# First batch laid out in memory already turned: its scores formed from the load, its other layout made on the chip

## The chip, the cores and the metric

The kernel runs on one core of a Trainium2 chip. The metric is the device time of one execution in microseconds (us), as the median of several executions. Five engines work from instruction queues of their own: PE (TensorE, matrix multiplies and turns), DVE (VectorE), ACT (ScalarE), POOL (GpSimd) and SP (SyncE, which here only issues transfers). Sixteen DMA engines move data between the chip's main memory and its SBUF.

## The reference

Eight batches of eight heads of attention between 512 tokens `x` and 32 states, in both directions, and then a soft mixture of eight experts over all 4608 rows.

```
scores  = scale * x @ state.T ;  a  = softmax(scores)  ; xread = a  @ state
scores2 = scale * state @ x.T ;  a2 = softmax(scores2) ; sread = a2 @ x
rows = concat(xread, sread), reshaped to (4608, 512)
logits = rows @ phi
slot_input = softmax(logits, over rows).T @ rows
slot_out[e] = relu(slot_input[e] @ w1[e]) @ w2[e]        # 8 experts, F = 1024
out = softmax(logits, over slots) @ slot_out
```

Everything is fp32. The weights are 32 MB of the some 42 MB that are read, and 8.9 MB are written.

## The kernel before

The attention is done one batch `b` at a time, and the batches overlap. The eight heads of a batch stand as four pairs `g`; `h` picks one of two halves. No scheduler decides the order: a hand-kept table `ORDER` lists steps by name (`X.0.1` is step `X` of batch 0, pair 1), each step issues its instructions when its turn comes, and every engine runs its own instructions strictly as they were issued. An instruction that waits holds up all that stand behind it on its engine.

The steps of one batch that matter here, with the lines of the kernel before:

- `X` (L228) turns one pair of the loaded `x` on PE (four 128x128 turns into a PSUM bank), and `xe` on ACT (L233) or `xd` on DVE (L238) copies the bank to SBUF times 0.125. The result is `xt`.
- `S` (L247) forms the scores of the batch on PE into two PSUM banks `sc` from the state and `xt`.
- First direction (softmax over the 32 states): `q` (DVE L260, a turn within 32x32 blocks out of `sc`), `m1` (DVE L265, maxima), `sub` (POOL L269), `x1` (ACT L272, exp), `l1` (DVE L276, sums), `rr` (DVE L281 and L282, one over the sums), `mul` (POOL L287), `aT` (DVE L292). Then `A`/`ae` turn and copy it, and `Lx` (PE L380) adds its logits.
- Second direction (softmax over the 512 tokens): `m2` (DVE L298, maxima out of `sc`), `e2` (ACT L303, exp with its sum), `E` (PE L311, a turn), `ee` on ACT or `ed` on DVE (L322, copy), `R` (PE L345, times `x` in its loaded layout), `sr` (DVE L358), `srT`, `srTe` (ACT) or `srTd` (DVE).
- `G` (PE L211) multiplies the states by `phi`, once for all batches. Its operand `phi_bd` is laid out by two copies on POOL (L203), which are issued ahead of the table and wait for the load of `phi`.
- `keep` copies logits out of PSUM, `V`/`Ve` turn and copy state results, `U`/`Ue` the states.

So `x` of a batch is used in two layouts: as loaded (tokens on partitions) by `R`, and turned by `S`. PSUM banks of `X`, `E`, `A`, `G` come from one pool of three (`ps_t`): a step that needs a bank waits for the copy that empties the one used three steps earlier.

SP issues the loads in one order: two of the four parts of `x` of batch 0 (256 KB each; ACT's queue issues the other two), the states of batches 0 and 1 (128 KB), `x` of batch 1 in two parts, the other states (384 KB), `phi` (64 KB), `x` of batches 2 to 7 (1 MB each), then the weights. `x` and weights share 13 SBUF buffers of 1 MB, and 4 of 2 MB hold weights; a weight that needs a buffer waits for the step that frees it (`load_w`).

After the attention come the experts: `w1` (PE L700), `w2` (PE L764), and the output (PE L800, copies on ACT L809 and DVE L810, stores issued by SP).

Of the kernel before, what the change touches and what calls it, by code (L numbers as in the profile page):

```python
# [35 lines left out]
l1.1.0 e2.2.0 R.1.0 sub.2.1 Lx.0.1 R.1.1 q.2.0 xe.3.2 X.3.3 rr.1 ae.0.0 A.0.1 X.4.3 e2.2.1 m1.2.0 sr.1 xe.3.3 S.3
xe.4.3 E.2.0 ae.0.1 mul.1.0 m2.3.1 aT.1.0 x1.2.1 X.4.0 mul.1.1 ee.2.0 X.4.1 E.2.1 xe.4.0 xe.4.1 q.3.1 X.4.2 sub.2.0
aT.1.1 srT.1 A.1.0 ee.2.1 x1.2.0 Lx.1.0 xe.4.2 R.2.0 Lx.1.1 R.2.1 m2.3.0 l1.2.1 l1.2.0 ae.1.0 mx.0 srTd.1 e2.3.0 mk.0
e2.3.1 X.5.2 keep.0 A.1.1 ae.1.1 rr.2 q.3.0 xe.5.2 sr.2 mul.2.1 E.3.0 bm.0 m1.3.0 nme.0 S.4 dx.0 X.5.0 ee.3.0 m1.3.1
sub.3.0 m2.4.1 aT.2.1 X.5.1 dT.0 E.3.1 m2.4.0 al.0 q.4.1 xe.5.0 dTe.0 x1.3.0 X.5.3 R.3.0 ee.3.1 T.0 e2.4.1 mul.2.0  # L40
aT.2.0 q.4.0 xe.5.3 Lu.0 R.3.1 srT.2 sub.3.1 m1.4.1 tt.0 sub.4.1 x1.3.1 xe.5.1 E.4.1 l1.3.0 A.2.0 l1.3.1 e2.4.0 m1.4.0
rr.3 x1.4.1 sub.4.0 X.7.2 Lx.2.0 ae.2.0 l1.4.1 ee.4.1 srTe.2 S.5 E.4.0 xe.7.2 X.7.1 sr.3 q.5.1 A.2.1 mul.3.0 ee.4.0
xe.7.1 ae.2.1 x1.4.0 m2.5.1 aT.3.0 m2.5.0 srT.3 X.7.3 srTe.3 xe.7.3 R.4.0 Lx.2.1 R.4.1 mul.3.1 aT.3.1 m1.5.1 sub.5.1
Lx.3.0 Ls.0 e2.5.0 X.7.0 e2.5.1 A.3.0 l1.4.0 q.5.0 Lse.0 E.5.0 rr.4 xe.7.0 Lr.0 A.3.1 x1.5.1 ee.5.0 ae.3.1 m1.5.0 S.7
msx.0 sub.5.0 dsx.0 sr.4 l1.5.1 ae.3.0 Lx.3.1 x1.5.0 mul.4.1 pv.1 m2.7.0 m2.7.1 R.5.0 l1.5.0 lkp.0 V.0 Ve.0 E.5.1 mx.1
ee.5.1 mul.4.0 rr.5 mul.5.1 U.0 srT.4 Ue.0 X.6.1 xe.6.1 X.6.0 R.5.1 srTd.4 q.7.1 mk.1 aT.4.0 sr.5 bm.1 nme.1 e2.7.0
xe.6.0 D.0 mul.5.0 aT.4.1 X.6.2 X.6.3 aT.5.0 E.7.0 srT.5 e2.7.1 xe.6.2 Px.0 xe.6.3 keep.1 q.7.0 m1.7.1 m1.7.0 E.7.1
ee.7.0 srTe.5 Y.0 S.6 Lx.4.0 sub.7.0 R.7.0 dx.1 m2.6.0 dT.1 ee.7.1 q.6.1 m2.6.1 aT.5.1 e2.6.0 sub.7.1 A.5.0 dTe.1
x1.7.0 m1.6.1 als.0 Lx.4.1 R.7.1 e2.6.1 al.1 q.6.0 Lx.5.0 T.1 x1.7.1 Lus.0 Lx.5.1 tt.1 windows E.6.0 ae.5.0 sub.6.1
keep.2 l1.7.0 m1.6.0 E.6.1 Ps.0 l1.7.1 Ys.0 A.4.0 ee.6.1 rr.7 ee.6.0 mx.2 sub.6.0 x1.6.1 pv.2 sr.7 A.5.1 l1.6.1  # L50
# [877 lines left out]
```

## Time and profile before

| | |
|---|---|
| time, median of 3 runs | 130.68 us (129.75 to 130.71) |
| time of the profiled execution | 130.03 us |
| its span, first to last instruction | 128.2 us |
| PE busy | 117.0 us (91%) |
| DVE busy | 86.4 us (67%) |
| ACT busy | 76.6 us (60%) |
| POOL busy | 44.8 us (35%) |
| moved by DMA | 51.74 MB, mean 404 GB/s |
| first instruction of the experts (PE L700) | at 76.11 us |

The span lies 1.83 us below the time of the same execution. Shares of busy time are means over three stages: the attention up to some 76 us, the experts up to some 100 us, and the output. The granted TensorE clock is 1.00 up to 122 us.

### The profile page before, as it was taken

The numbers are of one execution on the slowest core, as the hardware profiler recorded it, in microseconds if no ns is written. First come the engines' busy times: TensorE is split into PE (matmuls) and PEld (weight loads), VectorE is DVE, ScalarE is ACT, GpSimd is POOL, SyncE is SP. The second block draws the span as 40 slices with busy tenths as digits, with TensorE's granted clock in tenths as the row PEclk, the third lists the DMA queues.
The fourth block names the chain that finished last, engine by engine and source line by source line (L and its number), as shares of the span: only waits on it lengthen the run. The fifth ranks groups of instructions, "written<-read, shape, count | busy, mean of one in ns | idle before, by whom it ended". The sixth has DMA issues, their size and how long they took to land.

```text
span 128.2 us, 4689 instructions
## 1 busy us (share of the span) xinstructions
PE 117.0 (91%) x1984; PEld 81.2 (63%) x1984; DVE 86.4 (67%) x192; ACT 76.6 (60%) x187; POOL 44.8 (35%) x63
## 2 busy tenths in 40 slices
...
DVE  2329999999999999999985668029830346442600
...
DMA  3999999999999999999999999999999999999992
GB/s 138 396 409 430 419 429 419 429 419 427 419 422 427 419 427 424 419 427 422 427 422 429 419 415 409 431 414 434 414 447 414 414 380 413 432 399 416 373 414 105
DMA packets 8949, 51.74 MB, mean 404 GB/s; under 512 B 992, under 2 KB 1248, under 8 KB 4320
## 3 DMA queue, kind: packets, MB, share of 16 engines
...
q10 hardware_dynamic: 288, 0.52, 1.1%
...
## 4 chain that ended last, share of the span: by engine, by line
PE 70%; DVE 9%; DMA 7%; ACT 5%; issue 1%; DVEq 0%; POOL 0%; ACTq 0%; POOLq 0%
PE so_ps L764 12%; PE h_ps L700 11%; PE xt_ps L228 8%; PE o L800 7%; PE sc L247 5%; DMA phi_sb<-phi_in 5%; PE eT_ps L311 4%; PE sr_ps L345 4%; PE an_ps L311 3%; PE lt L380 3%; DMA x<-x_in 3%; PE t_ps L505 2%; DVE sums L276 2%; DVE q L260 2%; PE sum_ps L788 1%
## 5 line engine op out<-in xcount | busy, mean ns | idle before, releaser
L269 POOL TENSOR_TENSOR q<-q,m 128x512 f32<-128x512 f32 x16 | 16.8, 1051 | 15.6 <-DVE m L265 7.5
L233 ACT ACTIVATE xt<-xt_ps 128x512 f32<-128x512 f32 x30 | 17.9, 619 | 5.9 <-PE xt_ps L228 5.7
L228 PE MATMUL xt_ps<-ident,x 128*128 128x128 f32 x128 | 19.1, 291 | 0.0
L287 POOL TENSOR_TENSOR q<-q,rr 128x512 f32<-128x512 f32 x16 | 16.6, 1051 | 5.1 <-DVE rr L282 3.6
L810 DVE COPY out<-o 128x512 f32<-128x512 f32 x16 | 10.4, 686 | 11.5 <-PE o L800 11.4
L228 PEld LDWEIGHTS xt_ps<-ident,x 128*128 128x128 f32 x128 | 15.4, 150 | 3.0 <-ACT xt L233 0.8
L764 PE MATMUL so_ps<-w,h_m 128*32 128x128 f32 (+1 forms) x384 | 15.7, 310 | 0.0
L764 PEld LDWEIGHTS so_ps<-w,h_m 128*32 128x32 f32 x384 | 10.7, 110 | 7.4 <-issue 4.6
L700 PE MATMUL h_ps<-w,si_m 128*32 128x512 f32 x128 | 14.4, 594 | 0.1
L809 ACT COPY out<-o 128x512 f32<-128x512 f32 x16 | 8.7, 589 | 7.1 <-PE o L800 7.0
L298 DVE TENSOR_REDUCE nm<-sc 128x1 f32<-128x512 f32 x16 | 10.6, 671 | 2.7 <-PE sc L247 2.7
L700 PEld LDWEIGHTS h_ps<-w,si_m 128*32 128x32 f32 x128 | 9.1, 110 | 3.9 <-issue 2.9
L303 ACT ACTIVATE e<-sc,nm 128x512 f32<-128x512 f32 x16 | 11.3, 712 | 0.4 <-DVE nm L298 0.3
L260 DVE STREAM_TRANSPOSE q<-sc 128x512 f32<-128x512 f32 x16 | 11.1, 694 | 0.1
L292 DVE STREAM_TRANSPOSE aT<-q 128x512 f32<-128x512 f32 x16 | 10.9, 688 | 0.3 <-POOL q L287 0.2
L265 DVE TENSOR_REDUCE m<-q 128x16 f32<-128x512 f32 x16 | 10.4, 658 | 0.0
L276 DVE TENSOR_REDUCE sums<-q 128x16 f32<-128x512 f32 x16 | 10.4, 663 | 0.1
L272 ACT ACTIVATE q<-q 128x512 f32<-128x512 f32 x16 | 10.4, 649 | 0.1
L800 PE MATMUL o<-lt_all,so_r 32*128 32x512 f32 x64 | 10.2, 635 | 0.2 <-ACT out L809 0.2
L345 PE MATMUL sr_ps<-x,eT 128*32 128x64 f32 x512 | 10.4, 220 | 0.0
L311 PE MATMUL eT_ps<-ident,e 128*128 128x128 f32 x64 | 9.8, 279 | 0.0
L247 PE MATMUL sc<-xt,stT_sb 64*32 64x512 f32 x128 | 9.7, 601 | 0.0
...
## 6 DMA issues: line engine op xcount, KB each, us to landing
...
```

What stands on the lines that cost most here:

```text
L228: pe.transpose(p[:, P * j : P * j + P], xb[b][:, g, j, :], ident)
L233: act.mul(r[f"xt{g}"], r[f"xp{g}"], 0.125)
L247: pe.matmul(r[f"sp{h}"][32 * g : 32 * g + 32, :], st_t(b, g)[64 * h : 64 * h + 64, :], r[f"xt{g}"][64 * h : 64 * h + 64, :], start=True, s ...
L260: dve.transpose(r[f"q{h}"], r[f"sp{h}"])
L269: pool.tensor_tensor(v, v, R[b][f"m1{h}"].broadcast_to([P, 16, NS]), op=ALU.subtract)
L276: dve.tensor_reduce(out=v, in_=R[b][f"qv{h}"], axis=AX.X, op=ALU.add)
L287: pool.tensor_tensor(v, v, r.broadcast_to([P, 16, NS]), op=ALU.mult)
L311: pe.transpose(p[:, j, :], r[f"{src}{h}"][:, P * j : P * j + P], ident)
L345: pe.matmul(r["srp"][32 * g : 32 * g + 32, h, :], r[f"eT{h}"][:, j, 32 * g : 32 * g + 32], xb[b][:, g, j, D * h : D * h + D], start=(j == ...
L700: pe.matmul(h_ps[hf][32 * kt : 32 * kt + 32, :], si_m[kt // 2][:, 256 * (kt % 2) + 32 * e : 256 * (kt % 2) + 32 * e + 32], w1t[hf, e, kt], ...
L764: pe.matmul(so[k][32 * i : 32 * i + 32, :], h_m[hf][:, 256 * i + 32 * e : 256 * i + 32 * e + 32], w(i), start=(hf == 0 and e == 0), stop=( ...
L800: pe.matmul(o[j], so_r[hf][rows, col : col + 128], lt_all[rows, 4 * q : 4 * q + 4, :].rearrange("p b s -> p (b s)"), start=True, stop=True,)
```

## The change

Batch 0 is stored in main memory already turned (`x0T`: a pair's two heads times 64 on partitions, tokens along the row). A new step `S0` forms the scores of batch 0 from `x0T` as loaded, with states scaled by 0.125 on DVE (`st_s`); its first half takes pairs 0 and 1, its second pairs 2 and 3. The states of batches 0 and 1 are the first load, ahead of `x`. `X.0` turns `x0T` back, and `xe.0` copies it into a new SBUF buffer `x0`, from which `R.0` reads. That takes one of the 13 buffers, so one weight load fewer is issued ahead of the table, and the buffer of `x0T` takes that weight after the fourth `X.0`. A warm-up multiply `W0` on constants stands in front of the others. Copies by step: `xd` (DVE) goes from batch 0's pairs 1 and 0 to batch 1's pairs 3 and 2, batch 2's pair 1 and batch 6's pair 0; `ed.0.1` becomes `ee.0.1`, `keep.3` goes from ACT to DVE, `Ve.1` becomes `Vd.1`, `srTd` of batches 1 and 4 becomes `srTe`, and `srTe.0` becomes `srTd.0`. The whole table of steps is new.

```diff
 ORDER = """
-W.512 W.256 X.0.1 xd.0.1 X.0.0 xd.0.0 X.0.2 xe.0.2 X.0.3 xe.0.3 S.0 X.1.0 m2.0.1 X.1.2 X.1.1 xe.1.0 e2.0.1 xe.1.1
+W0.512 W.256 W.128 S0.0 S0.1 X.0.1 q.0.0 q.0.1 X.0.3 xe.0.1 X.0.0 xe.0.3 X.1.0 X.1.1 m1.0.0 m1.0.1 m2.0.0 sub.0.0
+xe.0.0 xe.1.0 m2.0.1 X.1.3 xe.1.1 X.1.2 sub.0.1 x1.0.0 xd.1.3 X.0.2 l1.0.0 e2.0.0 G.0 e2.0.1 G.3 G.1 x1.0.1 xd.1.2 G.2
...
     for b in range(B):
+        if b == 0:
+            nc.sync.dma_start(stT_sb[:, 0:1], st0)
+            x0T = big.tile([P, 4, S], F32, tag="big", name="x0T")
+            for i in range(4):
+                (act if i % 2 else nc.sync).dma_start(x0T[:, i], x0[i])
+            continue
         t = big.tile([P, 4, NJ, 2 * D], F32, tag="big", name=f"x{b}")
-        if b == 0:
-            for i in range(4):
-                v = x0[i].rearrange("p (g j c) -> p g j c", g=1, j=NJ)
-                (act if i % 2 else nc.sync).dma_start(t[:, 1 * i : 1 * i + 1], v)
-        elif b == 1:
+        if b == 1:
...
-        if b == 0:
-            nc.sync.dma_start(stT_sb[:, 0:1], st0)
...
+    xb.insert(0, big.tile([P, 4, NJ, 2 * D], F32, tag="big", name="x0"))
...
+    st_s = lt_all[:, B - 1, :].rearrange("p (a b n) -> p a b n", a=2, b=2)
+    dve.tensor_scalar_mul(st_s, stT_sb[:, 0, :, :, 0, :], 0.125)
...
             for j in range(NJ):
-                pe.transpose(p[:, P * j : P * j + P], xb[b][:, g, j, :], ident)
+                src = xb[b][:, g, j, :] if b else x0T[:, g, P * j : P * j + P]
+                pe.transpose(p[:, P * j : P * j + P], src, ident)
+            if b == 0:
+                r["turned"] = r.get("turned", 0) + 1
+                if r["turned"] == 4:
+                    load_w(1)
...
+        def xe(b, g, eng=act):
+            r = R[b]
+            if b == 0:
+                copy_of(eng)(xb[0][:, g].rearrange("p j c -> p (j c)"), r[f"xp{g}"])
+                return
...
+        def S0(i):
+            r = R[0]
+            for h in range(2):
+                if i == 0:
+                    r[f"sp{h}"] = ps_s.tile([P, S], F32, tag="sc", name=f"sc0_{h}")
+            for g in (2 * i, 2 * i + 1):
+                for h in range(2):
+                    pe.matmul(
+                        r[f"sp{h}"][32 * g : 32 * g + 32, :],
+                        st_s[64 * h : 64 * h + 64, g % 2, g // 2, :],
+                        x0T[64 * h : 64 * h + 64, g, :],
+                        start=True,
+                        stop=True,
+                    )
...
+        def first_warm(n):
+            p = ps_t.tile([P, S], F32, tag="tr", name="first_ps")
+            pe.matmul(p[:, 0:n], nc.const_aps.tensor(1.0, [P, P], F32), nc.const_aps.tensor(1.0, [P, n], F32), start=True, stop=True)
...
-        load_w(NBIG - B + 2 * NPAIR)
+        load_w(NBIG - B - 1 + 2 * NPAIR)
...
-        "x0_in": con(xl[0].reshape(P, 4, -1).transpose(1, 0, 2)),
+        "x0_in": con(x[0].reshape(4, 2, S, D).transpose(0, 1, 3, 2)).reshape(4, P, S),
```

How the instructions stand on three engines at the start of the attention follows, as they are issued, with what each waits for (PE, DVE, Activation and Pool are the engines; DMAHW is a transfer). `nm` is the result of `m2`, `m` of `m1`, `sums` of `l1`, `e` of `e2`.

DVE before, from its first work on data of batch 0:

```order
L238 TENSOR_SCALAR xt_1_165<-xt_ps_1_160 128x512 [waits PE_49]
L238 TENSOR_SCALAR xt_0_172<-xt_ps_0_167 128x512 [waits PE_49]
L298 TENSOR_REDUCE nm_0_1_203<-sc_1_189 128x1 [waits PE_49]
L260 STREAM_TRANSPOSE q_0_221<-sc_0_188 128x512
L298 TENSOR_REDUCE nm_0_0_242<-sc_0_188 128x1
L265 TENSOR_REDUCE m_0_0_252<-q_0_221 128x16 [waits DVE_49]
L260 STREAM_TRANSPOSE q_1_268<-sc_1_189 128x512 [waits Activation_49]
L265 TENSOR_REDUCE m_0_1_272<-q_1_268 128x16 [waits DVE_49]
L322 COPY eT_1_292<-eT_ps_1_259 128x512 [waits PE_49]
L276 TENSOR_REDUCE sums<-q_0_221 128x16 [waits Activation_49]
L298 TENSOR_REDUCE nm_1_0_312<-sc_0_282 128x1 [waits PE_49]
L260 STREAM_TRANSPOSE q_1_336<-sc_1_283 128x512 [waits PE_49]
```

DVE in the change, from its first work on scores of batch 0:

```order
L287 STREAM_TRANSPOSE q_0_177<-sc_0_162 128x512 [waits PE_49]
L287 STREAM_TRANSPOSE q_1_179<-sc_1_163 128x512 [waits PE_49]
L292 TENSOR_REDUCE m_0_0_203<-q_0_177 128x16 [waits DVE_49]
L292 TENSOR_REDUCE m_0_1_205<-q_1_179 128x16 [waits DVE_49]
L325 TENSOR_REDUCE nm_0_0_207<-sc_0_162 128x1
L325 TENSOR_REDUCE nm_0_1_213<-sc_1_163 128x1
L248 TENSOR_SCALAR xt_3_229<-xt_ps_3_215 128x512 [waits PE_49]
L303 TENSOR_REDUCE sums<-q_0_177 128x16 [waits Activation_49]
L248 TENSOR_SCALAR xt_2_269<-xt_ps_2_222 128x512 [waits PE_49]
L303 TENSOR_REDUCE sums<-q_1_179 128x16 [waits Activation_49]
L308 TENSOR_REDUCE rr_291<-sums 128x34 [waits DVE_49]
L309 RECIPROCAL rr_291<-rr_291 128x34 [waits DVE_49]
```

The two copies for batch 0 at the front are gone; both turns `q` and both `m1` come first; two copies for batch 1 (`xt_3`, `xt_2`) stand around the first `l1`, and both `l1` and `rr` of batch 0 stand ahead of all work on the scores of batch 1.

ACT before, from its first copy to the second exp of the first direction:

```order
L233 ACTIVATE xt_2_179<-xt_ps_2_174 128x512 [waits PE_49]
L233 ACTIVATE xt_3_186<-xt_ps_3_181 128x512 [waits PE_49]
L233 ACTIVATE xt_0_215<-xt_ps_0_198 128x512 [waits PE_49]
L303 ACTIVATE e_0_1_217,sums<-sc_1_189,nm_0_1_203 128x512 [waits DVE_49,Pool_49]
L233 ACTIVATE xt_1_219<-xt_ps_1_210 128x512 [waits PE_49]
L233 ACTIVATE xt_2_232<-xt_ps_2_205 128x512
L303 ACTIVATE e_0_0_264,sums<-sc_0_188,nm_0_0_242 128x512 [waits DVE_49]
L233 ACTIVATE xt_3_266<-xt_ps_3_254 128x512 [waits PE_49]
L272 ACTIVATE q_0_221<-q_0_221 128x512 [waits Pool_49]
L220 COPY G_sb<-g_ps 128x512 [waits PE_49]
L272 ACTIVATE q_1_268<-q_1_268 128x512 [waits Pool_49]
```

ACT in the change, from the same place:

```order
L242 COPY x_94<-xt_ps_1_172 128x512 [waits PE_49]
L242 COPY x_94<-xt_ps_3_181 128x512 [waits PE_49]
L242 COPY x_94<-xt_ps_0_187 128x512 [waits PE_49]
L246 ACTIVATE xt_0_211<-xt_ps_0_193 128x512 [waits PE_49]
L246 ACTIVATE xt_1_220<-xt_ps_1_198 128x512 [waits PE_49]
L299 ACTIVATE q_0_177<-q_0_177 128x512 [waits Pool_49]
L330 ACTIVATE e_0_0_239,sums<-sc_0_162,nm_0_0_207 128x512 [waits DVE_49]
L330 ACTIVATE e_0_1_250,sums<-sc_1_163,nm_0_1_213 128x512 [waits DVE_49]
L299 ACTIVATE q_1_179<-q_1_179 128x512 [waits Pool_49]
L224 COPY G_sb<-g_ps 128x512 [waits PE_49]
```

The first exp of the first direction, which waits for POOL, has moved ahead of both exps of the second direction, and the second one behind them.

POOL before, the two copies of `phi` and what stands behind them:

```order
L201 MEMSET phi_bd 128x256
L203 COPY phi_bd<-phi_sb 64x4x32 [waits DMAHW0_49,Pool_49]
L203 COPY phi_bd<-phi_sb 64x4x32
L269 TENSOR_TENSOR q_0_221<-q_0_221,m_0_0_252 128x512 [waits DVE_49,Pool_49]
L269 TENSOR_TENSOR q_1_268<-q_1_268,m_0_1_272 128x512 [waits DVE_49,PE_49]
```

POOL in the change, from the same place:

```order
L205 MEMSET phi_bd 128x256
L207 COPY phi_bd<-phi_sb 64x4x32 [waits DMAHW0_49,Pool_49]
L207 COPY phi_bd<-phi_sb 64x4x32
L296 TENSOR_TENSOR q_0_177<-q_0_177,m_0_0_203 128x512 [waits DVE_49,Pool_49]
L296 TENSOR_TENSOR q_1_179<-q_1_179,m_0_1_205 128x512 [waits DVE_49]
```

Nothing has moved there: the copies of `phi` stand in front of the first `sub` of batch 0 in both kernels.

## Rows read from the trace of the kernel before

**Rows 1.** The page of the profile, busy tenths in 40 equal slices of the span (3.2 us each), for VectorE and for the 16 DMA engines.

```profile
DVE  2329999999999999999985668029830346442600
...
DMA  3999999999999999999999999999999999999992
```

**Rows 2.** The view by windows, five stretches of the attention: window in us, its length, then busy us (and instructions) of PE, PEld, DVE, ACT and POOL, the granted TensorE clock, the busy share of the DMA engines, GB/s.

```profile
20.00:30.00 10.00, 10.00 (x216) 7.90 (x204) 9.70 (x19) 9.69 (x22) 5.55 (x6) 1.00 1.01 424
30.00:40.00 10.00, 10.00 (x219) 7.67 (x209) 9.93 (x23) 9.93 (x26) 5.49 (x7) 1.00 1.01 424
40.00:50.00 10.00, 10.00 (x210) 8.02 (x203) 9.93 (x23) 9.82 (x26) 6.98 (x7) 1.00 1.01 424
50.00:60.00 10.00, 9.98 (x232) 7.75 (x231) 9.86 (x24) 9.65 (x28) 5.80 (x9) 1.00 1.01 423
60.00:65.00 5.00, 4.68 (x95) 3.44 (x94) 4.83 (x15) 4.36 (x13) 4.25 (x5) 1.00 1.02 428
```

**Rows 3.** The chain of work that ended last, in order of time: start us, us, what.

```profile
3.97 6.09 DMA phi_sb<-phi_in
...
10.87 0.88 PE g_ps L211 x48
...
12.33 0.44 PE eT_ps L311 x4
...
13.13 1.07 PE sc L247 x16
...
64.45 0.30 DVE sr L358
...
70.82 0.27 ACT lt_all L390
...
76.11 9.06 PE h_ps L700 x80
```

**Rows 4.** The timeline of VectorE: start us, us, engine, line, operation, output and input, shapes, count, and in brackets the idle time before and what ended it.

```profile
5.18 0.69 DVE L238 TENSOR_SCALAR xt<-xt_ps 128x512 f32<-128x512 f32 x1 [2.89 <-PE xt_ps L228]
6.03 0.69 DVE L238 TENSOR_SCALAR xt<-xt_ps 128x512 f32<-128x512 f32 x1 [0.16 <-PE xt_ps L228]
...
9.12 0.69 DVE L298 TENSOR_REDUCE nm<-sc 128x1 f32<-128x512 f32 x1 [2.40 <-PE sc L247]
...
14.27 0.69 DVE L298 TENSOR_REDUCE nm<-sc 128x1 f32<-128x512 f32 x1
14.87 0.70 DVE L260 STREAM_TRANSPOSE q<-sc 128x512 f32<-128x512 f32 x1
15.50 0.64 DVE L276 TENSOR_REDUCE sums<-q 128x16 f32<-128x512 f32 x1
...
17.25 0.21 DVE L281 TENSOR_REDUCE rr<-sums 128x34 f32<-128x68 f32 x1
17.50 0.37 DVE L282 RECIPROCAL rr<-rr 128x34 f32<-128x34 f32 x1
17.79 0.66 DVE L260 STREAM_TRANSPOSE q<-sc 128x512 f32<-128x512 f32 x1
...
30.69 0.28 DVE L369 COPY srT<-srT_ps 128x128 f32<-128x128 f32 x1
30.88 0.21 DVE L281 TENSOR_REDUCE rr<-sums 128x34 f32<-128x68 f32 x1
```

**Rows 5.** The timeline of all engines, the same columns, rows of ScalarE and GpSimd between 10 and 14 us.

```profile
10.19 0.68 ACT L303 ACTIVATE e<-sc,nm 128x512 f32<-128x512 f32 x1
10.20 0.62 POOL L203 COPY phi_bd<-phi_sb 64x128 f32<-64x128 f32 x2 [8.49 <-DMA phi_sb<-phi_in]
...
10.86 1.09 ACT L233 ACTIVATE xt<-xt_ps 128x512 f32<-128x512 f32 x2
...
11.75 1.05 POOL L269 TENSOR_TENSOR q<-q,m 128x512 f32<-128x512 f32 x1 [0.94 <-DVE m L265]
...
12.95 0.67 ACT L272 ACTIVATE q<-q 128x512 f32<-128x512 f32 x1
...
13.47 0.62 ACT L220 COPY G_sb<-g_ps 128x512 f32<-128x512 f32 x1
```

**Rows 6.** The view of the transfers, issues by line: what, queue, operation, count, KB each, median us from issue to landing; and from the timeline the start of the issue of the states.

```profile
stT_sb<-st_in SPq DMA_DIRECT2D x1, 128.0 KB, 4.3
phi_sb<-phi_in SPq DMA_DIRECT2D x1, 64.0 KB, 6.1
...
1.63 0.42 SPq L98 DMA_DIRECT2D stT_sb<-st_in  x1
```

**Rows 7.** The timeline of TensorE: sixteen turns of batch 0, twelve of batch 1, and the scores of batch 1.

```profile
4.08 3.21 PE L228 MATMUL xt_ps<-ident,x 128*128 128x128 f32 x16
...
9.01 1.53 PE L228 MATMUL xt_ps<-ident,x 128*128 128x128 f32 x12
...
13.06 1.14 PE L247 MATMUL sc<-xt,stT_sb 64*32 64x512 f32 x16
```

**Rows 8.** The view by windows again, same columns as rows 2: four stretches from the first stores to the last.

```profile
100.00:105.00 5.00, 5.00 (x102) 2.97 (x102) 2.47 (x4) 2.41 (x5) 0.00 (x0) 1.00 0.94 397
105.00:110.00 5.00, 5.00 (x86) 2.94 (x88) 2.68 (x5) 2.57 (x6) 0.00 (x0) 1.00 0.99 408
...
115.00:120.00 5.00, 4.39 (x50) 2.35 (x42) 1.96 (x5) 2.72 (x8) 0.00 (x0) 1.00 0.94 383
120.00:122.00 2.00, 0.39 (x2) 0.00 (x0) 1.26 (x2) 1.00 (x2) 0.00 (x0) 1.00 1.02 418
```

More of the change, by code (lines that the diff above doesn't have):

```diff
@@ L36 @@
[L36 to L50, printed above, removed]
@@ new lines @@
+ae.0.1 aT.1.1 E.2.0 S.3 sr.1 sub.2.0 ee.2.1 X.4.0 sub.2.1 X.4.2 x1.2.0 srT.1 ee.2.0 aT.1.0 srTd.0 m2.3.0 l1.2.0 A.1.1
+x1.2.1 xe.4.0 X.4.1 l1.2.1 m2.3.1 Lx.1.0 q.3.1 xe.4.2 e2.3.0 ae.1.1 R.2.0 Lx.1.1 rr.2 xe.4.1 R.2.1 X.4.3 mx.0 srTe.1
+e2.3.1 xe.4.3 q.3.0 sr.2 mul.2.1 E.3.0 mul.2.0 mk.0 ee.3.0 A.1.0 E.3.1 m1.3.0 srT.2 aT.2.1 sub.3.0 bm.0 nme.0 S.4
+X.5.3 ae.1.0 aT.2.0 m1.3.1 keep.0 ee.3.1 q.4.1 m2.4.0 X.5.0 X.5.1 dx.0 x1.3.0 xe.5.3 srTe.2 sub.3.1 xe.5.1 dT.0 q.4.0
+m2.4.1 dTe.0 X.5.2 R.3.0 Lx.2.0 m1.4.0 x1.3.1 xe.5.0 m1.4.1 l1.3.0 l1.3.1 R.3.1 e2.4.0 sub.4.0 rr.3 e2.4.1 sr.3 Lx.2.1
```

41 lines of the change are left out of this document (25 added, 16 removed).

## The prediction

> **What bounds the kernel now.** I read the page's slices first. The DMA engines are full from the second slice to the last but one, and DVE is full from about 9 us until past 60 us [rows 1]. The windows say it closer: from 20 to 65 us DVE is busy 9.70 to 9.93 of every 10 us and 4.83 of the last 5, while PE (as the profile models it) and ACT stand nearly as high [rows 2]. The idle time of DVE in these 45 us is 0.30 + 0.07 + 0.07 + 0.14 + 0.17 = 0.75 us. So in the attention the time is the work that DVE has, plus the moment at which it starts; whatever is added to DVE, or left idle on it early, arrives almost undiminished at 65 us. The chain of waits agrees at its turning point: DVE's `sr` at 64.45 us releases the tail of the attention, and `w1` starts at 76.11 us [rows 3].
>
> At the end a second bound stands close by. The first store follows the last load so closely that the DMA engines are busy 0.94 of 100 to 105 us, 0.99, later 0.94, and 1.02 [rows 8]. A delay of the first store leaves them idle for as long, and the end moves with it. An advance gains only what they now miss: 5 x 0.06 + 5 x 0.01 + 5 x 0.06 = 0.65 us. By bytes, against the 424 GB/s of the attention [rows 2], the same three windows miss 5 x (27 + 16 + 41) / 424 = 1.0 us. These two are the bounds of any gain.
>
> **What the change gives.** Before, DVE has two copies at 5.18 and 6.03 us and then idles 2.40 us until the scores are there at 9.12 us [rows 4]. After, the scores need only the loads. The same five transfers must land; the last of them landed at 1.63 + 4.3 = 5.93 us [rows 6], now it is a part of `x0T`. Behind it stands half of `S0`. A whole `S` takes 1.14 us, and early work of PE runs at about half the later pace (16 turns in 3.21 us against 12 in 1.53 us [rows 7], at a granted clock of 1.00), so half costs 0.6 to 1.1 us. DVE gets its first `q` at 6.5 to 7.0 us; I take 6.8, 2.3 us earlier. The scaling of the states on DVE and `W0` lie in the wait for the loads and cost nothing; without that cover each would cost under 1 us, which the next step hides as well.
>
> **What takes it back: POOL.** The first `sub` needs `m1`, but on POOL the two copies of `phi` stand ahead of it, before and after. `phi` is issued at 3.97 us and lands 6.09 us later, at 10.06 us [rows 3]; the copies take 0.62 us from 10.20 us [rows 5]. The change moves no bytes from in front of `phi` to behind it. So `sub` starts at about 10.85 us, against 11.75 before. Before, little was queued behind this wait: ACT and DVE had `e2`, `m2` and copies to do. After, they have not:
>
> - DVE runs `q`, `q`, `m1`, `m1`, `m2`, `m2` and one copy at a pitch of 0.60 us (14.27, 14.87, 15.50 [rows 4]), from 6.8 to 11.0 us. Next in its queue is `l1.0.0`, which needs `x1.0.0`, which needs `sub`: 10.85 + 1.05 + 0.52 = 12.45 us (1.05 of `sub`; 0.52 is `x1` at 12.95 to the next at 13.47 [rows 5]). DVE idles 1.45 us.
> - Behind `l1.0.0` stands the copy of `xt` of batch 1, pair 2, from 13.05 to 13.7 us, and PE's scores of batch 1 wait for it. They run 13.75 to 14.9 us; before, they ended at 13.06 + 1.14 = 14.20 us [rows 7].
> - ACT has `x1.0.0` ahead of both `e2` now. So `x1.0.1` waits for two `e2` of 0.67 us each (10.19 to 10.86 [rows 5]): 12.45 + 1.35 + 0.52 = 14.35 us. Then `l1.0.1` can go, then `rr`, and at 15.5 us the first turn on scores of batch 1. DVE idles another 0.7 us in front of `l1.0.1`.
>
> If the cover is priced the other way: with `sub` free to go when `m1` is there (8.65 us), the same walk puts `l1.0.0` at 11.0 us without idling and the first turn of batch 1 at 13.4 us. The wait for `phi` is worth 2.1 us of DVE's time.
>
> **The ledger at 15.5 us.** Before, DVE starts `l1.0.1` at 15.50 us and has `m2.1.0` and a `q` of batch 1 behind it [rows 4]. After, it has done `l1.0.1` (0.60) and `rr` (17.25 to 17.79, 0.54 [rows 4]) which before had not; it still owes `m2.1.0` and that `q` (1.20), and two copies `xd` that before sat on ACT (batches 2 and 6: 1.20); it is spared one `srTd` (30.69 to 30.88, 0.19 [rows 4]). Sum: 1.20 + 1.20 - 0.60 - 0.54 - 0.19 = 1.07 us more work, from the same moment on, on an engine with 0.75 us of idle time in the rest. PE gives the same: its scores of batch 1 end 0.7 us later and one turn of 0.44 us [rows 3] that was done before is still owed, 1.1 us. ACT owes about the same as before, and is later spared some copies; it doesn't set the end.
>
> The rest of the change: the four `X.0` and their four copies exist in both kernels; their later use, `R.0`, comes after `S.1` in both. The buffer that `x0` takes costs one weight load issued ahead, which now waits for the fourth `X.0`, about 10.5 us, while SP's queue reaches it far later, with all of `x` and twelve weights in front of it; no cost, and up to the 2.4 us by which a megabyte fills the engines at 424 GB/s if that cover were gone. In the tail `keep.3` leaves ACT, where it takes 0.27 us of the chain [rows 3]: -0.27. `Vd.1` falls into DVE's slack behind 65 us [rows 1]. The experts and the output are untouched.
>
> **Sum.** 1.07 - 0.27 = +0.8 us at the start of the experts, and as much at the end. The profiled execution of before took 130.03 us, 0.65 below the median; the three runs and it have a mean of 130.3 us. By the profiled one alone 130.8 us, by the median 131.5 us; I go from the mean: 131.1 us.
>
> [...] The row says that 64 KB of `phi` took 6.1 us to land where 128 KB of states issued earlier took 4.3 us [rows 6]. [...]
>
> **Rivals.**
>
> *Faster: POOL is not held.* If `phi` lands by 8.0 us, `sub` is free at `m1`'s end and the 2.1 us come back: DVE ends 1.05 us earlier than before, the experts start 1.3 us earlier, and the DMA engines let through 0.65 to 1.0 us: 129.3 to 129.65 us, I write 129.5. For it: the states in front are small, and the page doesn't show why a transfer lands when it does. Against: the same bytes stand in front of `phi`. Chance 0.17.
>
> *No difference.* The table is new throughout; behind batch 1 it may fill the 0.75 us of idle time, or batch 0's early `m1` may spare later waits. It would give 130.3 us. For it: three engines share the load almost evenly [rows 2], so an order can shift work; ACT has the room. Against: DVE has nothing to fill. The case that the early scores change nothing at all lies here too. Chance 0.23.
>
> *More stalls.* Four copies on DVE now hold PSUM banks for PE, and each stands behind a reduction that waits for POOL or ACT. The two that I walked cost 1.45 and 0.7 us; a further one (batch 2, pair 1, before `S.2`) costs about one `sub`, 1.05 us: 132.1 us. It decides from the point at which `S.2` waits for that copy. Chance 0.20.
>
> *The forecast*, +0.3 to +1.5 us, 130.6 to 131.8 us: 0.40.
>
> **Chances and range.** About 1% (1.3 us) is what a measurement can tell from no change: under 129.4 is faster, over 132.0 slower. Faster is a good half of the first rival, 0.10. Slower is most of the stalls and a tail of the forecast, 0.22. The rest, 0.68, is within 1%. The range goes from the first rival's 129.5 to 132.5, the stalls with some of their spread; it leaves out under a tenth on each side.
>
> **What would show it.** Right: DVE's first `q` near 6.8 us; POOL's first `sub` still at 10.8 us behind `phi`; an idle time of DVE over 1 us in front of the first `l1` and a second one in front of the next; scores of batch 1 not earlier than before; DVE's last `sr` about 1 us later, `w1` starting near 76.9 us. Wrong: `phi` landing at 9 us or earlier, or DVE without idle time between 7 and 15 us; `w1` starting before 76 us; or a start of `w1` that moves without the end moving, which would put the bound into the DMA engines instead.

## The result and the profile after

| | before | after |
|---|---|---|
| median, 20 runs each | 130.31 us (129.52 to 131.73) | 131.19 us (130.60 to 131.58) |
| time of the profiled execution | 130.03 us | 131.54 us |
| its span | 128.2 us | 129.8 us |
| VectorE busy | 86.4 us | 88.1 us |
| first instruction of the experts | 76.11 us | 78.11 us |

The changed kernel takes 1.0069 of the time before, 95% interval 1.0047 to 1.009: slower by 0.9 us in the medians, which the 1% of the prediction counts as no change. The two profiled executions stand further apart, 1.51 us: that of before is 0.28 us under its median, that of after 0.35 us over its own. Ratios here and below leave out three executions in a slower state, one of e1 and two of e2, which the medians of those two runs include.

VectorE (DVE) after, its timeline from the first work on scores to the first turns of batch 1, then its last `sr` (columns as in [rows 4]):

```profile
8.07 1.31 DVE L287 STREAM_TRANSPOSE q<-sc 128x512 f32<-128x512 f32 x2 [3.95 <-PE sc L260]
9.30 1.24 DVE L292 TENSOR_REDUCE m<-q 128x16 f32<-128x512 f32 x2
10.46 1.28 DVE L325 TENSOR_REDUCE nm<-sc 128x1 f32<-128x512 f32 x2
11.65 0.68 DVE L248 TENSOR_SCALAR xt<-xt_ps 128x512 f32<-128x512 f32 x1
13.17 0.69 DVE L303 TENSOR_REDUCE sums<-q 128x16 f32<-128x512 f32 x1 [0.84 <-ACT q L299]
13.78 0.68 DVE L248 TENSOR_SCALAR xt<-xt_ps 128x512 f32<-128x512 f32 x1
15.03 0.69 DVE L303 TENSOR_REDUCE sums<-q 128x16 f32<-128x512 f32 x1 [0.57 <-ACT q L299]
15.75 0.22 DVE L308 TENSOR_REDUCE rr<-sums 128x34 f32<-128x68 f32 x1
16.00 0.37 DVE L309 RECIPROCAL rr<-rr 128x34 f32<-128x34 f32 x1
16.29 1.25 DVE L287 STREAM_TRANSPOSE q<-sc 128x512 f32<-128x512 f32 x2
...
66.08 0.29 DVE L385 TENSOR_TENSOR sr<-sr_ps,rr 128x128 f32<-128x128 f32 x1
```

The scores reach DVE 1.05 us earlier than the 9.12 us of [rows 4]. Then the two idle times that were forecast stand in front of the two `l1`, 0.84 and 0.57 us, and the turns of batch 1 start at 16.29 us. The last `sr` is 1.63 us later than in [rows 3].

What the two idle times wait for, first on GpSimd (POOL), then on ScalarE (ACT), timelines of after:

```profile
10.72 0.61 POOL L207 COPY phi_bd<-phi_sb 64x128 f32<-64x128 f32 x2 [9.02 <-DMA phi_sb<-phi_in]
11.43 2.06 POOL L296 TENSOR_TENSOR q<-q,m 128x512 f32<-128x512 f32 x2
```

```profile
12.51 0.63 ACT L299 ACTIVATE q<-q 128x512 f32<-128x512 f32 x1 [0.64 <-POOL q L296]
13.05 0.67 ACT L330 ACTIVATE e<-sc,nm 128x512 f32<-128x512 f32 x1
...
13.71 0.68 ACT L330 ACTIVATE e<-sc,nm 128x512 f32<-128x512 f32 x1
...
14.37 0.62 ACT L299 ACTIVATE q<-q 128x512 f32<-128x512 f32 x1
```

POOL does nothing until `phi` is there, although DVE had done both `m1` by 10.54 us; the first `sub` follows the copies at 11.43 us. The second exp of the first direction stands behind both of the second direction.

TensorE (PE), timeline of after: the scores of batch 0 from the load, and those of batch 1.

```profile
5.31 2.68 PE L260 MATMUL sc<-x0T,lt_all 64*32 64x512 f32 x16 [1.21 <-DMA x0T<-x_in]
...
13.86 1.76 PE L274 MATMUL sc<-xt,stT_sb 64*32 64x512 f32 x16 [0.25 <-ACT e L330]
```

The new step takes 2.68 us. The scores of batch 1 start 0.80 us later than before [rows 7].

The windows of after, columns as in [rows 2] and [rows 8]:

```profile
20.00:30.00 10.00, 9.76 (x174) 7.04 (x164) 9.96 (x21) 9.35 (x22) 5.59 (x6) 1.00 1.01 424
30.00:40.00 10.00, 10.00 (x231) 8.23 (x233) 9.81 (x20) 10.00 (x28) 4.88 (x5) 1.00 1.01 424
40.00:50.00 10.00, 10.00 (x202) 7.12 (x199) 9.76 (x24) 9.81 (x25) 6.29 (x7) 1.00 1.01 421
50.00:60.00 10.00, 10.00 (x196) 7.75 (x195) 9.96 (x23) 9.10 (x26) 5.40 (x7) 1.00 1.01 425
60.00:65.00 5.00, 4.80 (x137) 3.61 (x136) 4.97 (x13) 4.91 (x11) 2.98 (x3) 1.00 1.01 423
100.00:105.00 5.00, 4.78 (x88) 2.80 (x80) 1.58 (x3) 1.87 (x5) 0.00 (x0) 1.00 0.84 357
...
115.00:120.00 5.00, 4.62 (x79) 2.69 (x70) 1.29 (x2) 1.98 (x5) 0.00 (x0) 1.00 1.00 408
```

DVE now idles 0.54 us of the 45 (0.04 + 0.19 + 0.24 + 0.04 + 0.03), against 0.75 before: no slack is left for a late start. In the output the first stores come later (0.84 of 100 to 105 us where it was 0.94 in [rows 8]), and the stretch before the end, 0.94 before, is now full.

The chain of after, in order of time:

```profile
4.05 6.54 DMA phi_sb<-phi_in
...
66.47 2.06 POOL q L314 x2
68.56 0.72 DVE aT L319
...
78.11 9.06 PE h_ps L731 x80
```

It starts from `phi`, as that of before did [rows 3]. New in it are two `mul` on POOL, which start 0.39 us behind the last `sr`; that `sr`, on which the chain of before turned, does not stand in it, since the pair waits for a copy on ACT (L361). From `sr` to the experts it is 12.03 us, where it was 11.66.

### The profile page after: what moved, and what is told of

Read it like the earlier page. It is cut to its first block, busy times and chain, and to the rows that moved or that the text cites. A ratio compares the mean times of both kernels' runs of the same rounds, so it can differ in the third digit from the quotient of the medians.

```text
span 129.8 us, 4693 instructions
## 1 busy us (share of the span) xinstructions
PE 118.2 (91%) x1986; PEld 80.5 (62%) x1986; DVE 88.1 (68%) x195; ACT 75.8 (58%) x185; POOL 44.7 (34%) x63
## 4 chain that ended last, share of the span: by engine, by line
PE 46%; DVE 28%; DMA 8%; ACT 5%; POOL 3%; issue 3%; DVEq 0%; ACTq 0%; POOLq 0%
PE so_ps L795 11%; PE h_ps L731 11%; PE o L831 7%; DVE q L287 6%; DVE nm L325 5%; DVE sums L303 5%; DMA phi_sb<-phi_in 5%; DVE aT L319 4%; DVE m L292 4%; DMA x0T<-x_in 3%; PE an_ps L338 2%; PE sc L274 2%; POOL q L296 2%; POOL q L314 2%; PE t_ps L532 2%
## 5 line engine op out<-in xcount | busy, mean ns | idle before, releaser
L233 PE MATMUL xt_ps<-ident,x 128*128 128x128 f32 x112 | 15.4, 278 | 0.0
L246 ACT ACTIVATE xt<-xt_ps 128x512 f32<-128x512 f32 x24 | 14.0, 607 | 0.2 <-DVE aT L319 0.2
L233 PEld LDWEIGHTS xt_ps<-ident,x 128*128 128x128 f32 x112 | 12.3, 140 | 2.5 <-ACT lt_all L417 0.8
L372 PEld LDWEIGHTS sr_ps<-x,eT 128*32 128x32 f32 x512 | 8.4, 110 | 2.0 <-issue 1.5
```

What stands on the lines that cost most here:

```text
L233: pe.transpose(p[:, P * j : P * j + P], src, ident)
L372: pe.matmul(r["srp"][32 * g : 32 * g + 32, h, :], r[f"eT{h}"][:, j, 32 * g : 32 * g + 32], xb[b][:, g, j, D * h : D * h + D], start=(j == ...
```

## The experiments

The theory taken to the chip: DVE's full stretch hands on any delay, and what the early scores bring is taken back (1) by POOL, which holds the first `sub` behind the copies of `phi`, and (2) by the copies that the change adds to DVE. Rivals: (3) the scores are simply not early enough, because PE is slow in the new step; (4) the loss sits in the order of DVE's copies around `l1`; (5) it sits in the tail. Every ratio is to the kernel before on the same chip; the changed kernel was timed in the first comparison only, so an edit of it is set against it through the two ratios. The columns after the ratio are of the profiled execution, in us. "First turn" is the start of batch 1's first `q` in kernels with the change, and of `l1.0.1` in the others, the moment from which the prediction made its ledger; "stretch" is from there to the last `sr`.

| run | median | ratio (95%) | DVE's first work on scores | first `sub` | first turn | last `sr` | stretch | experts | span |
|---|---|---|---|---|---|---|---|---|---|
| before | 130.31 | 1 | 9.12 | 11.75 | 15.50 | 64.45 | 48.95 | 76.11 | 128.2 |
| after | 131.19 | 1.0069 (1.0047 to 1.009) | 8.07 | 11.43 | 16.29 | 66.08 | 49.79 | 78.11 | 129.8 |
| e1_phi_early | 130.77 | 1.0026 (0.9992 to 1.0059) | 8.07 | 10.11 | 15.12 | 64.92 | 49.80 | 76.93 | 128.6 |
| e2_pool_order | 130.39 | 0.9989 (0.9955 to 1.0024) | 8.16 | 10.13 | 15.33 | 65.13 | 49.80 | 76.81 | 128.6 |
| e9_warm_only | 131.28 | 1.0101 (1.0065 to 1.0136) | 7.09 | 11.10 | 15.96 | 65.76 | 49.80 | 77.78 | 129.4 |
| e6_pool_warm | 130.22 | 1.0018 (0.9993 to 1.0043) | 7.17 | 9.14 | 14.03 | 64.00 | 49.97 | 75.96 | 128.4 |
| e5_copies_act | 131.86 | 1.0133 (1.0112 to 1.0153) | 7.20 | 11.14 | 16.00 | 66.39 | 50.39 | 78.39 | 130.1 |
| e7_all | 130.19 | 1.0011 (0.9998 to 1.0025) | 7.44 | 9.40 | 14.30 | 64.89 | 50.59 | 76.73 | 128.4 |
| e3_xd_first | 131.08 | 1.0083 (1.0054 to 1.0112) | 8.14 | 10.83 | 15.69 | 65.48 | 49.79 | 77.51 | 129.2 |
| e8_tail_act | 131.65 | 1.0127 (1.0105 to 1.0148) | 8.05 | 10.48 | 15.84 | 65.64 | 49.80 | 78.26 | 129.9 |
| e4_before_phi_early | 129.69 | 0.9962 (0.9937 to 0.9986) | 8.27 | 10.90 | 14.98 | 63.94 | 48.96 | 75.63 | 127.8 |
| e10_before_w0 | 130.16 | 1.0001 (0.9985 to 1.0017) | 8.45 | 11.34 | 15.94 | 64.84 | 48.90 | 76.69 | 128.5 |
| e11_before_w0_phi | 129.75 | 0.9967 (0.9955 to 0.9979) | 8.65 | 11.28 | 15.16 | 64.13 | 48.97 | 76.25 | 128.0 |

### POOL let go of `phi`

e1_phi_early: the change, with `phi` loaded right behind the parts of `x0T`.

```diff
             for i in range(4):
                 (act if i % 2 else nc.sync).dma_start(x0T[:, i], x0[i])
+            nc.sync.dma_start(phi_sb, phi)
             continue
...
-            nc.sync.dma_start(phi_sb, phi)
```

> The changed kernel, with the load of phi issued right behind the four parts of x of batch 0, ahead of batch 1. Theory A (the early gain is lost because the first sub stands on POOL behind the copies of phi): phi lands near 7 us, the first sub starts when m1 is there, near 10.0 us instead of 11.43, DVE's idle times of 0.84 and 0.57 us in front of the two l1 go, DVE's last sr comes 1.2 to 1.4 us earlier, the end 0.8 to 1.3 us earlier than the changed kernel, about 130.1 us. Theory B (the loss is the two copies xd of batches 2 and 6 that DVE was given): the idle times may go, but the end moves by less than 0.3 us. Theory C (the loss is the late first scores, 8.07 us, because TensorE works at half pace there): less than 0.3 us too.

e2_pool_order: the change, with the two copies of `phi` issued behind both `sub` instead of ahead of the table.

```diff
-        for h in range(2):
-            pool.tensor_copy(phi_bd[64 * h : 64 * h + 64, :, h, :], phi_sb[64 * h : 64 * h + 64])
...
         def G(i):
             if "gp" not in R[0]:
+                for h in range(2):
+                    pool.tensor_copy(phi_bd[64 * h : 64 * h + 64, :, h, :], phi_sb[64 * h : 64 * h + 64])
```

> The changed kernel, with the two copies of phi issued on POOL behind the first two subs of batch 0 instead of ahead of them; no load is moved. Theory A: sub starts near 10.0 us, both subs are done near 12.1, the copies of phi follow until 12.7 and G of PE starts near 12.8 instead of 12.5 us, which costs nothing since the scores of batch 1 wait for DVE's copy; gain as with the early load of phi, 0.8 to 1.3 us. Theories B and C: under 0.3 us.

POOL and DVE of e1, then of e2, from their timelines:

```profile
6.36 0.61 POOL L207 COPY phi_bd<-phi_sb 64x128 f32<-64x128 f32 x2 [4.65 <-DMA phi_sb<-phi_in]
10.11 2.06 POOL L296 TENSOR_TENSOR q<-q,m 128x512 f32<-128x512 f32 x2 [3.14 <-DVE m L292]
```

```profile
10.13 2.06 POOL L296 TENSOR_TENSOR q<-q,m 128x512 f32<-128x512 f32 x2 [8.43 <-DVE m L292]
12.13 0.63 POOL L210 COPY phi_bd<-phi_sb 64x128 f32<-64x128 f32 x2
```

```profile
14.07 0.69 DVE L303 TENSOR_REDUCE sums<-q 128x16 f32<-128x512 f32 x1 [0.45 <-ACT q L299]
...
15.33 1.25 DVE L287 STREAM_TRANSPOSE q<-sc 128x512 f32<-128x512 f32 x2
...
65.13 0.29 DVE L385 TENSOR_TENSOR sr<-sr_ps,rr 128x128 f32<-128x128 f32 x1
```

In both, `sub` now waits for `m1` of DVE and for nothing else, the idle time before the first `l1` is gone, and the first turn moves 1.17 and 0.96 us ahead of 16.29 us. The stretch behind it keeps its 49.80 us, so the last `sr` moves by as much (1.16 and 0.95). In time e2 gives back 1.0069 - 0.9989 = 0.8%, 1.0 us, and e1 0.4%, 0.6 us; the interval of e2 lies clear of that of the change, that of e1 overlaps it, and its gain is under the 0.8 to 1.3 us expected. e2 moves more than the front: its tail is shorter too (below). So `phi` does hold the changed kernel, by 0.4 to 0.8% of its time, and without that hold the change is level with before, not ahead. Whether this sets the two kernels apart is another question, which e4 below answers.

### Earlier scores

e9_warm_only: the change with a longer warm-up ahead of the new step, so that PE is busy for longer before it.

```diff
-W0.512 W.256 W.128 S0.0 S0.1 X.0.1 q.0.0 q.0.1 ...
+W0.512 W.512 W.256 S0.0 S0.1 X.0.1 q.0.0 q.0.1 ...
```

> The changed kernel with the longer warm-up multiplies alone; POOL's copies of phi stay ahead of the first sub. Theory A: DVE's first q starts near 7.2 instead of 8.07 us, but the first sub still waits for phi (10.8 to 11.4 us), so DVE only idles longer in front of the first l1 (1.4 us or more, for 0.84), the first turn of batch 1 stays at 15.9 to 16.3 us, and the end within 0.3 us of the changed kernel. Theory C (late scores cost the time themselves): the end comes 0.6 to 0.9 us earlier.

Timeline of DVE in e9:

```profile
7.09 1.31 DVE L287 STREAM_TRANSPOSE q<-sc 128x512 f32<-128x512 f32 x2 [3.18 <-PE sc L260]
...
12.85 0.69 DVE L303 TENSOR_REDUCE sums<-q 128x16 f32<-128x512 f32 x1 [1.49 <-ACT q L299]
```

The scores are 0.98 us earlier, and the idle time in front of `l1` has grown from 0.84 to 1.49 us: nothing arrives at the end (1.0101). While `phi` holds the `sub`, theory (3) falls.

e6_pool_warm: e2 with that warm-up, both at once.

> The changed kernel with the copies of phi on POOL behind the first two subs (as in the run before), and with longer warm-up multiplies (512, 512 and 256 columns for 512, 256 and 128), which fill the 1.1 to 1.3 us that PE idles ahead of the first scores. Theory C (first scores late because PE works at half pace, 1056 ns for a multiply that later takes 601): with the gap filled the scores run at full pace, DVE's first q starts near 7.2 instead of 8.16 us, and with POOL free that arrives at the end: 0.6 to 1.0 us below the run with the POOL order alone, about 129.5 us. Rival: the pace does not depend on the gap, or the longer warm-up holds the scores up: within 0.3 us of that run.

Timeline of DVE in e6:

```profile
7.17 1.31 DVE L287 STREAM_TRANSPOSE q<-sc 128x512 f32<-128x512 f32 x2 [3.38 <-PE sc L260]
...
12.74 0.69 DVE L303 TENSOR_REDUCE sums<-q 128x16 f32<-128x512 f32 x1
...
14.03 1.31 DVE L287 STREAM_TRANSPOSE q<-sc 128x512 f32<-128x512 f32 x2
...
64.00 0.29 DVE L385 TENSOR_TENSOR sr<-sr_ps,rr 128x128 f32<-128x128 f32 x1
```

The windows from DVE's first work on scores to the end of its last `sr`, before and then e6 (columns as in [rows 2]):

```profile
9.12:64.74 55.62, 55.10 (x1143) 42.48 (x1143) 54.69 (x117) 53.59 (x132) 33.23 (x38) 1.00 1.01 423
```

```profile
7.17:64.29 57.12, 56.08 (x1157) 43.10 (x1156) 56.23 (x117) 53.88 (x131) 30.82 (x33) 1.00 1.01 423
```

At the first turn the earlier scores count: no idle time is left in front of either `l1`, and the first turn comes 2.26 us ahead of the change's. The forecast for the time was a miss all the same: 130.22 us, level with before. DVE starts on scores 1.95 us earlier than before and ends its last `sr` only 0.45 us earlier: it needs 64.00 - 7.17 = 56.83 us where before it needed 64.45 - 9.12 = 55.33. The 1.50 us between them are added work, as (2) has it: DVE is busy 56.23 us there against 54.69, and idle 0.89 against 0.93. Of the remaining 0.45 us the tail, 11.96 against 11.66 us, takes another 0.30. The experts start 0.15 us ahead of those of before, and yet the span ends 0.2 us later; against e2 they start 0.85 us earlier and the span is 0.2 us shorter. So most of what the earlier scores bring is lost behind the attention, and in time e6 is no faster than e2 (1.0018 and 0.9989).

### The added copies, and their order

e5_copies_act: the change, with the added copies of batches 2 and 6 back on ACT. e7_all: e6 with the same edit.

```diff
-... R.0.1 e2.1.1 m1.1.0 x1.1.1 xd.2.1 sr.0 l1.1.1
+... R.0.1 e2.1.1 m1.1.0 x1.1.1 xe.2.1 sr.0 l1.1.1
...
-xd.6.0 R.5.1 ...
+xe.6.0 R.5.1 ...
```

> The changed kernel, with the copies of batch 2, pair 1, and batch 6, pair 0, back on ACT (xe.2.1, xe.6.0 for xd.2.1, xd.6.0). DVE's stretch from its first turn of batch 1 to its last sr was 49.79 us in the changed kernel and in each of the three edits of it so far, against 48.95 us from the same point of the ledger in the kernel before. Theory B (the work term of the ledger: two copies at 0.60 us): the stretch shrinks by 1.0 to 1.2 us, to 48.6 to 48.8 us, and the end by 0.7 to 1.0 us. Rival: ACT is as full as DVE (9.4 to 10.0 of 10 us), takes 0.98 us more and holds DVE up in turn: the stretch shrinks by less than 0.4 us.

> All three edits together: copies of phi behind the first two subs, longer warm-up, the two copies of batches 2 and 6 on ACT. If the three terms add (0.8 to 1.0, 0.6 to 1.0, 0.7 to 1.0 us), the attention ends near 74.5 us against 76.11 of the kernel before, and the DMA engines cap what arrives at the end: 128.7 to 129.4 us, faster than both kernels by 0.5 to 1.1%. If DMA caps harder or ACT takes over: within 0.3 us of the run with two edits.

Timeline of DVE in e5, and two of its windows:

```profile
7.20 1.31 DVE L287 STREAM_TRANSPOSE q<-sc 128x512 f32<-128x512 f32 x2 [3.19 <-PE sc L260]
...
12.88 0.69 DVE L303 TENSOR_REDUCE sums<-q 128x16 f32<-128x512 f32 x1 [1.41 <-ACT q L299]
...
20.84 0.69 DVE L303 TENSOR_REDUCE sums<-q 128x16 f32<-128x512 f32 x1 [0.44 <-ACT q L299]
...
22.33 0.69 DVE L303 TENSOR_REDUCE sums<-q 128x16 f32<-128x512 f32 x1 [0.19 <-ACT q L299]
```

```profile
30.00:40.00 10.00, 10.00 (x229) 8.24 (x226) 9.96 (x21) 10.00 (x28) 4.98 (x5) 1.00 1.00 420
40.00:50.00 10.00, 10.00 (x201) 7.10 (x201) 9.76 (x24) 10.00 (x26) 6.29 (x7) 1.00 1.02 426
```

Both are misses. The stretch grows by 0.6 us instead of shrinking by the 1.2 us of two copies (50.39 and 50.59 against 49.79 and 49.97). DVE is spared work (from its first turn to the end of its last `sr` it is busy 48.66 us in e5, 49.36 in after), but is idle for 2.02 us there instead of 0.72. Its longest waits in e5 are for ACT's exps, 0.6 us in all, and for scores and turns of PE; ACT is busy for 20.00 of the 20 us from 30 to 50, against 19.81 in after. In this table ACT seems to have no room for the two copies either. So (2) holds as a sum of work, but no edit of these steps undoes it, and that the added copies cost the time is argued from the busy time, not shown.

e5 shows one thing more that was not planned. Its front is that of the change, and yet its scores came at 7.20 us in the profiled execution, 0.87 us earlier than in that of after; the idle time in front of `l1` was 1.41 us, the `sub` came at 11.14 us, and the first turn 0.29 us earlier, as its `sub` was.

e3_xd_first: the change, with the second copy for batch 1 ahead of the first `l1`.

```diff
-... x1.0.0 xd.1.3 X.0.2 l1.0.0 e2.0.0 G.0 e2.0.1 G.3 G.1 x1.0.1 xd.1.2 G.2
+... x1.0.0 xd.1.3 xd.1.2 X.0.2 l1.0.0 e2.0.0 G.0 e2.0.1 G.3 G.1 x1.0.1 G.2
```

> The changed kernel, with DVE's copy of batch 1, pair 2, placed ahead of the first l1 instead of behind it; POOL still waits for phi. Theory A in its second half (the copy is queued behind a waiting l1, and the scores of batch 1 with it): the copy runs near 12.2 us instead of 13.78, the scores of batch 1 end 1.0 to 1.4 us earlier, near 14.4 us, DVE's first idle time shrinks from 0.84 to 0.2 us; but the second l1 still waits for ACT's exp, so the time gained is 0.3 to 0.8 us. Theories B and C: no change.

A miss: 1.0083 against 1.0069. The timeline of DVE has the first idle time gone and the second grown from 0.57 to 0.79 us:

```profile
14.43 0.69 DVE L303 TENSOR_REDUCE sums<-q 128x16 f32<-128x512 f32 x1 [0.79 <-ACT q L299]
...
15.69 1.25 DVE L287 STREAM_TRANSPOSE q<-sc 128x512 f32<-128x512 f32 x2
```

The first turn is 0.60 us earlier than in after, but in this execution POOL's `sub` was 0.60 us earlier too (10.83 against 11.43); the edit itself adds nothing. From `sub` to first turn it is 4.86 us in both: that way runs over ACT's four exps, not over DVE. While `phi` holds the `sub`, theory (4) falls.

### The tail

e8_tail_act: the change with `keep.3` and `Ve.1` on ACT, as before.

```diff
-... aT.6.1 Vd.1 Lx.6.0 ...
+... aT.6.1 Ve.1 Lx.6.0 ...
-... mkd.3 keepd.3 dsx.1 ...
+... mkd.3 keep.3 dsx.1 ...
```

> The changed kernel, with keep.3 and the copy of V.1 back on ACT as in the kernel before. The forecast's tail term (keep.3 off ACT is worth 0.27 us): the stretch from DVE's last sr to w1 grows from 12.03 to about 12.3 us. Rival: both copies are off the path in this table, or cost DVE as much as they spare ACT: the stretch stays within 0.15 us of 12.03, or falls towards the 11.66 us of the kernel before.

From `sr` at 65.64 us to the experts at 78.26 it is 12.62 us, 0.59 more than in the change. So the two moves do shorten the tail, by more than was forecast, and (5), put down to them, falls. What makes the new tail longer than the old one must be something else. A pair of `mul` on POOL stands near its start, here before, then after, then in e2:

```profile
64.49 2.06 POOL L287 TENSOR_TENSOR q<-q,rr 128x512 f32<-128x512 f32 x2 [0.26 <-ACT dx L477]
```

```profile
66.47 2.05 POOL L314 TENSOR_TENSOR q<-q,rr 128x512 f32<-128x512 f32 x2 [1.30 <-ACT an L361]
```

```profile
65.17 2.06 POOL L314 TENSOR_TENSOR q<-q,rr 128x512 f32<-128x512 f32 x2 [0.94 <-DVE rr L309]
```

Before, POOL starts this pair 0.04 us behind DVE's last `sr`; after, 0.39 us behind it, released by an ACT copy, and the chain runs through it. From the start of the pair to the experts it is 11.62 us before, and 11.63 or 11.64 in after, e1, e2, e3, e5 and e9: the late pair is 0.35 of the 0.37 us. In e2, e6 and e7, which leave `phi`'s copies for later, it starts 0.03 to 0.05 us behind `sr` and is not in the chain; the tail takes 11.68 us in e2, but 11.96 and 11.84 in e6 and e7. So 0.35 us of what e2 gains at the experts over after comes from the tail. Why the pair waits for ACT's copy in one order of POOL and not in the other is open, and no run moved it alone.

### The kernel before, with the same two levers

e4_before_phi_early: before, with `phi` right behind the first states. e10_before_w0: before, with the warm-up of the change. e11_before_w0_phi: both.

```diff
         if b == 0:
             nc.sync.dma_start(stT_sb[:, 0:1], st0)
+            nc.sync.dma_start(phi_sb, phi)
...
-            nc.sync.dma_start(phi_sb, phi)
```

```diff
-W.512 W.256 X.0.1 xd.0.1 ...
+W0.512 W.256 W.128 X.0.1 xd.0.1 ...
```

> The kernel before, with the load of phi issued right behind x of batch 0 and the states, ahead of batch 1. Theory A: phi is covered there, DVE has other work from 9.12 us on and no idle time; only PE's 0.34 us in front of G and the first sub (11.75 us, whose m1 is done at 11.6) are near it: within 0.3 us of the kernel before. If this gains as much as the same edit gives the changed kernel, phi is a cost of both kernels and explains no difference between them.

> The kernel before, with the warm-up of the change alone (constants first: 512, 256 and 128 columns, from 0.77 us on instead of 1.36). If the pace of PE at the start costs the kernel before time, its first scores come earlier than 9.12 us, near 8.3, and the end up to 0.5 us earlier; if phi at 10 us and DVE's later work hide it, the same within 0.2 us.

> The kernel before with the same warm-up and with phi loaded ahead of batch 1. Early phi alone gave a ratio of 0.9962 to the kernel before. If the two work on the same wait, 129.6 to 129.8 us again; if they add, 129.2 to 129.5 us, a version faster than both kernels.

The earlier `phi` gives 0.4% with or without the warm-up (129.69 and 129.75 us, both intervals under 1): the fastest versions of this study, ahead of both kernels. e4 was expected within 0.3 us of the kernel before; it gains 0.5 us by its ratio. The text recorded for e4 says what equal gains would mean, and they are equal: the same edit gives 0.4% in the changed kernel (e1) and 0.4% in the kernel before. With `phi` early in both, on the same chip, the change still is slower, 1.0026 against 0.9962, with intervals that don't overlap: 0.64%, where the first comparison had 0.69%. On these numbers `phi` is a cost of both kernels, and most of the difference between them lies elsewhere. In the profiled executions of e1 and e4 the experts start 1.30 us apart: 0.14 us at the first turn, 0.84 in the stretch (DVE is busy 49.36 us there against 48.45), 0.32 in the tail.

The warm-up alone gives nothing. Nor does a run show that it brings the scores forward, since e4 without it has them at 8.27 us, e10 with it at 8.45. The timeline of DVE in e10 shows where its earlier scores went:

```profile
13.24 0.69 DVE L322 COPY eT<-eT_ps 128x512 f32<-128x512 f32 x1 [0.97 <-PE eT_ps L311]
```

That copy waits for turns on PE that stand in PE's queue behind `G`, and `G`, in front of which PE idles 0.79 us, needs `phi`, whose copies on POOL start at 10.63 us there. Once its scores come early, `phi` holds the kernel before as well, on another engine.

## Why the prediction was right in time, and what was off in its steps

The forecast was +0.8 us at the end; the medians differ by 0.88 us. The mechanism was the one forecast in two points: the early scores bring nothing to the first turn, since POOL is held behind `phi`, and the added work of DVE arrives at its last `sr`. One premise was wrong: that little was queued behind the wait for `phi` in the kernel before. Freed of it, that kernel gains 0.4% (e4) as the changed one does (e1), so most of the difference lies in the ledger and the tail. That the sum came within 0.1 us is in part luck, for several terms were off, in both directions, and the profiled pair shows them: +0.79 at the first turn (forecast 0), +0.84 in the stretch (1.07), +0.37 in the tail (-0.27), together 2.00 at the experts (0.8), and -0.4 behind them (0).

- **What bounds it** was right. From the first turn to the last `sr` it is 49.79 or 49.80 us in after, e1, e2, e3, e8 and e9, with first turns from 15.12 to 16.29 us: a shift in front is handed on to 0.01 us.
- **DVE's first `q`**: 6.5 to 7.0 us was too early; 8.07. The term that failed is the pace of the new step: half of it, behind the last part of `x0T`, was put at 0.6 to 1.1 us. The last part came when forecast (the weight loads of the second half wait for it until 6.05 us, forecast 5.93), but the step ended at 7.99, 1.9 us later; in e5, at the faster pace, it was 1.06. The rows gave a weaker slowdown than the prediction read: 3.21 us for 16 turns against 1.53 for 12 is 1.6 times, not double. While `phi` holds the `sub` the late scores cost no time: e9 has them at 7.09 us and ends no earlier than after. But it halved the price of the hold: with `q` at 8.1 us, `sub` could go at 10.1 at the earliest (e1, e2), not at 8.65.
- **POOL and `phi`**: the mechanism was right (e1, e2, e9); the size was off. `phi` was put at 10.06 us, it landed at 4.05 + 6.54 = 10.59, the first `sub` was 0.58 us late against the forecast, and the way from there to the first turn took 4.86 us where 4.65 was worked out: together the 0.79 us. The forecast summed 2.15 us of idle time and measured 1.41, the rest being the late `q`. In the runs that leave `phi` in its place (after, e3, e5, e8, e9) the copies start at 10.72, 10.13, 10.44, 9.78 and 10.40 us; that of after is the latest, 0.32 over their median. Since such delays are handed on, this would be most of the 0.35 us by which the profiled execution lies over the median of after.
- **The ledger**: 1.07 forecast, 49.79 - 48.95 = 0.84 measured, and the same between e1 and e4, where `phi` holds no `sub` (49.80 against 48.96). Its reason can be put more simply than the prediction did. The two copies taken off DVE lay in its idle time in front of the scores [rows 4] and had cost nothing; the four put on it lie behind the first scores, two of them in the full stretch. Four at the pitch of 0.60 us, less `ed.0.1` (0.60) and one `srTd` (0.19), are an estimate of 1.61 us; e6, with nothing to wait for in front, took 1.50 us longer, 1.54 by its busy time.
- **The tail**: -0.27 was forecast, +0.37 measured. The term itself had the right sign and was too small (e8: the two moves give 0.59); the step that failed is the silent one, that the rest of the new table leaves the tail as it was. There the `mul` pair starts 0.35 us later behind `sr`; why is open.
- **The end**: a delay was to move it by as much. Of 2.00 us at the experts 1.6 arrived in the span. The output's transfers had gaps to give: 115 to 120 us went from 0.94 [rows 8] to 1.00.
- **The landing of `phi`**: issued at 4.05 us behind the large loads (after), it took 6.54 us; issued at 2.10 us in e1 and e4, with `x` of batch 1 behind it and not ahead, it took 4.1 and 4.0. That agrees with the ground on which the forecast kept the landing of before, that the same bytes stand in front of `phi`; what holds the landing up, no run shows.

The rivals. *POOL is not held* did not happen; `phi` came later, not earlier. Its price was wrong too: e2 and e6 build that case, and it gives the time of the kernel before (0.9989 and 1.0018) instead of 0.8 us less. The start gains less (first turn at 14.03 us at best, forecast 13.4), the tail is longer by 0.30 us in e6 where 0.27 less was forecast, and 0.35 us are lost behind the experts. *No difference* failed at its reason: DVE's idle time in the full stretch shrank by 0.21 us only. *More stalls* did not come: no idle time of that size stands in the windows from 20 us on.
